# Two last output tiles: one 128-row store each in place of two 64-row stores

## The chip, the cores and the metric

The kernel runs on one core of one Trainium2 chip. The metric is device time in microseconds for one execution, as the median of several runs. The engines of the core have names of their own in the profile: PE is TensorE (matmuls), ACT is ScalarE, DVE is VectorE, POOL is GpSimd and SP is SyncE. SyncE and ScalarE each have a queue from which they issue transfers between the on-chip memory (SBUF) and device memory. The transfers are carried out by 16 DMA engines that the queues share.

## The reference

An attention block with sketched polynomial features is followed by a feed-forward block with the ELU activation. Only the last lines matter for the change, but the whole is short:

```python
# q, k, v: (4, 4, 1088, 32) float32; S1, S2: (8, 32)
def phi(x):                                   # 64 features from 32 numbers
    a = einsum('rd,bhsd->bhsr', S1, x)
    b = einsum('rd,bhsd->bhsr', S2, x)
    return einsum('bhsi,bhsj->bhsij', a, b).reshape(..., 64)
q_p, k_p = phi(q), phi(k)
kv = einsum('bhsf,bhsd->bhfd', k_p, v)
z = sum(k_p, axis=2)
attn = einsum('bhsf,bhfd->bhsd', q_p, kv) / (einsum('bhsf,bhf->bhs', q_p, z)[..., None] + 1e-06)

x = attn.transpose(0, 2, 1, 3).reshape(4352, 128)
h = x @ w_in                                  # w_in (128, 2048)
g = where(h > 0, h, exp(minimum(h, 0)) - 1)
out = g @ w_out                               # w_out (2048, 128), out (4352, 128) float32
```

## The kernel before

The 4352 rows of the output are held as 4 batches of 64 x 17 rows: row (b, y, t) with y from 0 to 63 and t from 0 to 16. A "half tile" is one (b, t), 64 rows that lie 17 rows apart in the output. There are 68 half tiles, in nine groups g of eight; the last group (g = 8) has only four. Its two output tiles of 128 rows are the last work of the kernel.

```python
NT = S // 64                                   # 17
NH = B * NT                                    # 68 half tiles
NQ = (NH + 7) // 8                             # 9 groups
qn = [min(8, NH - 8 * g) // 2 for g in range(NQ)]   # tiles of a group: 4, the last group 2

def half_tile(g, k):
    return divmod(8 * g + k, NT)
# ... cut ...
def halves(dst, lhs, rhs, **kw):               # one product as two matmuls of 64 output rows
    for u in range(2):
        nc.tensor.matmul(dst[64 * u:64 * u + 64], lhs[:, 64 * u:64 * u + 64], rhs, skip_group_check=True,
                         tile_position=(0, 64 * u), **kw)
# ... cut ...
def mm2_last(cp, first, last):                 # second product of the last group: rows on the partitions
    g = NQ - 1
    if first:
        ops[g] = [psum.tile([P, P], F32, name="ol", tag=t, bufs=k) for t, k in (("o0", 1), ("aux", 2))]
    gg = gs.pop((g, cp))
    for a in range(4):
        c, i = (a % 2, a // 2) if last else divmod(a, 2)
        halves(ops[g][i][:], gg[:, c, i * P:i * P + P], W[:, cp, (2 + c) * P:(3 + c) * P],
               start=(first and c == 0), stop=(last and c == 1))

def fin_last():                                # copy out of PSUM, and store
    g, n = NQ - 1, qn[NQ - 1]
    o = work.tile([P, 2, P], F32, name="ol", tag="ol", bufs=1)
    rows = out.rearrange("(b y t) f -> b y t f", b=B, t=NT)
    for i, copy in enumerate((nc.scalar.copy, nc.vector.tensor_copy)):
        copy(o[:, i, :], ops[g][i][:])
        for u, eng in enumerate((nc.sync, nc.scalar)):
            b, t = half_tile(g, u * n + i)
            eng.dma_start(rows[b, :, t, :], o[64 * u:64 * u + 64, i])
```

In the last step (cp = 7) the matmuls of tile i = 0 come before those of tile i = 1, so the first copy, on ScalarE, can begin while the second tile is still being summed. The earlier groups are stored by SyncE alone, from tiles named ob.

ScalarE issues only three other transfers, all at the start of the kernel. S2 goes to the tile raw_s, eight rows of 256 B. The second half of the first k goes to the tile hd_k, and a half of the first queries goes to hd_q:

```python
def load_hd(eng, x, src, b, t0, t1, c=slice(0, 2)):
    # ... cut ...
    eng.dma_start(hd[x, b][:, c, t0:t1, :],
                  src[b].rearrange("h (a c t) d -> (h a) c t d", a=32, c=2)[:, c, t0:t1, :])
# ... cut ...
for x, (eng, src) in enumerate(((nc.sync, S1), (nc.scalar, S2))):
    rs = slice(R * x, R * x + R)                             # R = 8
    # ... cut ...
    eng.dma_start(raw_s[rs].rearrange("p c w -> p (c w)"), src.bitcast(U32))
load_hd(nc.sync, "k", k, 0, 0, KT)                           # KT = 9
load_hd(nc.scalar, "k", k, 0, KT, NT)
load_hd(nc.sync, "q", q, 0, 0, 8, slice(0, 1))
load_hd(nc.scalar, "q", q, 0, 0, 8, slice(1, 2))
```

Of the kernel before, what the change touches and what calls it, by code (L numbers as in the profile page):

```python
# [27 lines left out]
def kernel(  # L28
# [21 lines left out]
    nc = tc.nc  # L50
# [413 lines left out]
    def half_tile(g, k):  # L464
        return divmod(8 * g + k, NT)
# [372 lines left out]
    def fin_last():  # L838
        g, n = NQ - 1, qn[NQ - 1]
        o = work.tile([P, 2, P], F32, name="ol", tag="ol", bufs=1)  # L840
        rows = out.rearrange("(b y t) f -> b y t f", b=B, t=NT)
        for i, copy in enumerate((nc.scalar.copy, nc.vector.tensor_copy)):
            copy(o[:, i, :], ops[g][i][:])
            for u, eng in enumerate((nc.sync, nc.scalar)):
                b, t = half_tile(g, u * n + i)
                eng.dma_start(rows[b, :, t, :], o[64 * u:64 * u + 64, i])


    for t0, t1 in ((0, 5), (KT, KT + 5), (5, KT), (KT + 5, NT)):
# [143 lines left out]
    for n in range(2, N + 2):  # L993
        if n < N:
            g, cp = steps[n]
# [26 lines left out]
        g, cp = steps[n - 2]  # L1022
# [5 lines left out]
        elif n > 2:  # L1028
            mm2(g, cp, cp == 0, cp == NP - 1)
            if cp == NP - 1:  # L1030
                fin1(g)
    fin_last()


# [27 lines left out]
```

## Time and profile before

| what | value |
|---|---|
| time, median of 3 runs | 268.3 us (267.77 to 268.83) |
| span of the profiled execution | 266.5 us |
| PE busy | 260.4 us, 98% |
| DVE busy | 187.7 us, 70% |
| ACT busy | 183.9 us, 69% |
| POOL busy | 159.6 us, 60% |
| DMA packets, whole run | 26418, 13.60 MB |
| of these on q1, SyncE's queue | 25792 |
| of these on q10, ScalarE's queue | 592 |

The profile is of one execution; its span is a little shorter than the time measured from outside. Times inside it are counted from the start of the span. A line such as L846 is the line of the kernel from which an instruction comes. In this kernel L843 is the copy in fin_last and L846 its store. SPq and ACTq are the instruction queues of SyncE and ScalarE, where issues of transfers and waits are seen. "To landing" is the time from the issue of a transfer to the last of its completion signals. A packet is one contiguous run that a DMA engine moves, or the small write by which it signals completion.

### The profile page before, as it was taken

The numbers are of one execution on the slowest core, as the hardware profiler recorded it, in microseconds if no ns is written. First come the engines' busy times: TensorE is split into PE (matmuls) and PEld (weight loads), VectorE is DVE, ScalarE is ACT, GpSimd is POOL, SyncE is SP. The second block draws the span as 40 slices with busy tenths as digits, with TensorE's granted clock in tenths as the row PEclk, the third lists the DMA queues.
The fourth block names the chain that finished last, engine by engine and source line by source line (L and its number), as shares of the span: only waits on it lengthen the run. The fifth ranks groups of instructions, "written<-read, shape, count | busy, mean of one in ns | idle before, by whom it ended". The sixth has DMA issues, their size and how long they took to land.

```text
span 266.5 us, 7686 instructions
## 1 busy us (share of the span) xinstructions
PE 260.4 (98%) x3115; PEld 154.9 (58%) x3115; DVE 187.7 (70%) x346; ACT 183.9 (69%) x355; POOL 159.6 (60%) x233
## 2 busy tenths in 40 slices
PE   8899999999999999999999999999999999999994
PEld 6743323343333665667576666666766666666884
DVE  6799999996969796996647867554346444673652
ACT  2378978686566575786567777777777777777782
POOL 4400007303505985798859799898688888898300
PEclk9999999999999999999999999999999999999999
DMA  5997960001001300001100110001000100010011
GB/s 192 320 349 215 270 197 17 0 21 65 2 0 28 57 1 2 2 2 19 27 5 0 21 22 2 0 12 25 10 1 15 27 4 1 14 19 12 2 27 35
DMA packets 26418, 13.60 MB, mean 51 GB/s; under 512 B 19216, under 2 KB 24592, under 8 KB 26384
## 3 DMA queue, kind: packets, MB, share of 16 engines
q1 hardware_dynamic: 25792, 12.66, 18.5%
q8 instruction: 24, 0.39, 0.6%
q10 hardware_dynamic: 592, 0.46, 0.5%
q14 instruction: 10, 0.08, 0.1%
HBM read 10.88 MB, written 2.23 MB: 49 GB/s over the span
## 4 chain that ended last, share of the span: by engine, by line
PE 93%; DVE 4%; POOL 1%; issue 1%; ACT 0%; DVEq 0%
PE h L226 43%; PE pb L730 16%; PE pa L730 12%; PE o L226 11%; PE ol L226 3%; PE idle L231 2%; PE kv L391 1%; PE h L648 1%; PE qps L648 1%; DVE qp L586 1%; POOL kp L287 1%; PE kfps L323 1%; PE qps L542 1%; PE kv L226 1%; PE abp L304 1%
## 5 line engine op out<-in xcount | busy, mean ns | idle before, releaser
L799 DVE SCALAR_TENSOR_TENSOR gg<-e,h 128x512 f32<-128x512 f32 (+1 forms) x144 | 92.3, 653 | 64.2 <-ACT e L793 62.9
L226 PE MATMUL h<-xg,W 128*64 128x512 f32 (+1 forms) x584 | 128.7, 563 | 0.0
L791 ACT ACTIVATE e<-h 128x512 f32<-128x512 f32 (+1 forms) x144 | 81.4, 565 | 50.6 <-PE h L226 48.1
L793 ACT ACTIVATE e<-e 128x512 f32<-128x512 f32 (+1 forms) x144 | 87.5, 607 | 4.4
L226 PEld LDWEIGHTS h<-xg,W 128*64 128x64 f32 x584 | 40.1, 137 | 47.4 <-issue 36.8
L710 POOL TENSOR_TENSOR tt<-gg 128x256 f32<-128x256 f32 x48 | 35.1, 730 | 16.4 <-DVE gg L799 16.0
L713 POOL TENSOR_TENSOR tt<-gg 128x256 f32<-128x256 f32 x48 | 35.3, 736 | 14.4 <-DVE gg L799 14.0
L715 POOL TENSOR_TENSOR tt<-gg,tt 128x256 f32<-128x256 f32 x48 | 36.5, 760 | 3.8
L714 POOL TENSOR_TENSOR tt<-tt,gg 128x256 f32<-128x256 f32 x48 | 35.2, 733 | 3.8
L730 PEld LDWEIGHTS pa<-gg,W 128*64 128x64 f32 x384 | 23.6, 137 | 22.7 <-issue 22.0
L226 PE MATMUL o<-gg,W 128*64 128x512 f32 x128 | 30.5, 597 | 0.4 <-DVE W L129 0.4
L730 PE MATMUL pa<-gg,W 128*64 128x128 f32 x384 | 29.5, 275 | 0.0
L730 PE MATMUL pb<-tt,SS 128*64 128x128 f32 x384 | 29.1, 273 | 0.0
L730 PEld LDWEIGHTS pb<-tt,SS 128*64 128x64 f32 x384 | 22.6, 137 | 0.0
L126 POOL TENSOR_TENSOR raw<-raw,tiny 128x512 f32<-128x512 f32 x1 | 1.0, 1039 | 29.8 <-DVE raw L121 29.8
L730 PE MATMUL pb<-gg,SS 128*64 128x128 f32 x192 | 18.7, 273 | 0.0
L730 PE MATMUL pa<-tt,SS 128*64 128x128 f32 x192 | 18.6, 273 | 0.0
L730 PE MATMUL pb<-tt,W 128*64 128x128 f32 x192 | 18.6, 273 | 0.0
L226 PEld LDWEIGHTS o<-gg,W 128*64 128x64 f32 x128 | 8.5, 136 | 16.2 <-issue 13.8
L730 PEld LDWEIGHTS pb<-tt,W 128*64 128x64 f32 x192 | 12.1, 137 | 0.0
L730 PEld LDWEIGHTS pa<-tt,SS 128*64 128x64 f32 x192 | 12.1, 137 | 0.0
L730 PEld LDWEIGHTS pb<-gg,SS 128*64 128x64 f32 x192 | 12.1, 137 | 0.1
(150 smaller groups left out, 245.0 us busy)
## 6 DMA issues: line engine op xcount, KB each, us to landing
raw<-in_moe_w_in_dram SPq DMA_DIRECT2D x8, 256.0 KB, 5.8
raw<-in_moe_w_out_dram SPq DMA_DIRECT2D x8, 256.0 KB, 5.8
hd_k<-in_k_dram SPq DMA_DIRECT2D x3, 544.0 KB, 7.8
hd_q<-in_q_dram SPq DMA_DIRECT2D x3, 544.0 KB, 3.2
v<-in_v_dram SPq DMA_DIRECT2D x4, 288.0 KB, 6.4
out_dram<-ob SPq DMA_DIRECT2D x72, 16.0 KB, 1.5
v<-in_v_dram SPq DMA_DIRECT2D x4, 256.0 KB, 7.5
out_dram<-ob SPq DMA_DIRECT2D x16, 32.0 KB, 1.7
```

Source lines behind the costliest of these rows:

```text
L226: nc.tensor.matmul(dst[64 * u:64 * u + 64], lhs[:, 64 * u:64 * u + 64], rhs, skip_group_check=True, tile_position=(0, 64 * u), **kw)
L231: nc.tensor.matmul(idle[:, :cols], some[:, :P], some[:, :cols], skip_group_check=True)
L287: eng.tensor_mul(dst, _ap(a_, list(a_.ap[1:]) + [[0, R]]), _ap(b_, [b_.ap[1], [0, R], b_.ap[2]]))
L648: nc.tensor.matmul(ps[w][s * r:s * r + s, 64 * k:64 * (k + m)], lhs, qpT[g, i][rows, o + 2 * k:o + 2 * (k + m), f, :], start=(f == 0 and j ...
L710: nc.gpsimd.tensor_tensor(t[:, 0], b12, b11, op=SUB)
L713: nc.gpsimd.tensor_tensor(t[:, 2], b22, b12, op=SUB)
L714: nc.gpsimd.tensor_tensor(t[:, 1], t[:, 2], b11, op=ADD)
L715: nc.gpsimd.tensor_tensor(t[:, 3], b21, t[:, 1], op=SUB)
L730: nc.tensor.matmul(bank[64 * u:64 * u + 64, P * col:P * col + P], lhs, rhs[:, u], start=(first and i in (0, 3)), stop=last, skip_group_che ...
L791: nc.scalar.activation(e, hs[g, cp][c][:, :n], RELU, scale=-1.0)
L793: nc.scalar.activation(e, e, EXP, scale=-1.0)
L799: nc.vector.scalar_tensor_tensor(gs[g, cp][:, c, :n], es[g, cp][:, c, :n], -1.0, hs[g, cp][c][:, :n], op0=ADD, op1=MAX)
```

## The change

Before, each of the two last tiles is stored in two halves of 64 rows, the half u = 0 by SyncE and the half u = 1 by ScalarE: four transfers, two on each queue. After, each tile is stored by one transfer of 128 rows: the first, which ScalarE has copied, by ScalarE, and the second, which VectorE has copied, by SyncE. Two issues on the two queues fall away, and SyncE has nothing in front of the last store. The two halves of a tile lie n = 2 values of t apart in the output, so the destination is written as (u, y, f), with u outermost.

```diff
         o = work.tile([P, 2, P], F32, name="ol", tag="ol", bufs=1)
         rows = out.rearrange("(b y t) f -> b y t f", b=B, t=NT)
-        for i, copy in enumerate((nc.scalar.copy, nc.vector.tensor_copy)):
+        for i, (copy, eng) in enumerate(((nc.scalar.copy, nc.scalar), (nc.vector.tensor_copy, nc.sync))):
             copy(o[:, i, :], ops[g][i][:])
-            for u, eng in enumerate((nc.sync, nc.scalar)):
-                b, t = half_tile(g, u * n + i)
-                eng.dma_start(rows[b, :, t, :], o[64 * u:64 * u + 64, i])
+            b, t = half_tile(g, i)
+            eng.dma_start(rows[b, :, t:t + n + 1:n, :].rearrange("y u f -> u y f"), o[:, i])
```

Nothing else in the kernel is changed.

## The prediction

> **What bounds the kernel now.** I read the profile's page first. It says that the matmul engine carries the run: 98% busy over the span, 93% of the chain that ended last. The change touches none of that. It only touches the last two stores, so the question is what lies between the last matmul and the end of the span, and whether the stores set that end. The chain of work in order of time, cut to the last microseconds, answers half of it (columns: start, duration, what):
>
> ```profile
> 260.32 2.64 PE ol L226 x48
> 262.96 0.02 issue
> 262.99 0.29 DVE ol L843
> ```
>
> The chain stops at the second copy, which ends at 262.99 + 0.29 = 263.28 us. The span ends at 266.5 us. So 3.2 us come after the last arithmetic. The timeline of the same stretch shows who starts the stores, and the sync engine's own waits show what it waits for after that (waited for: us in total, times, longest):
>
> ```profile
> 262.55 0.27 ACT L843 COPY ol<-ol 128x128 f32<-128x128 f32 x1 [1.06 <-PE ol L226]
> 262.84 1.19 SPq L846 DMA_DIRECT2D out_dram<-ol  x2
> 262.84 1.46 ACTq L846 DMA_DIRECT2D out_dram<-ol  x2
> ```
>
> ```profile
> SPq L1058 <- DMA out_dram<-ol: 1.4, 2, 1.2
> ```
>
> L1058 is the end of the program. SyncE sits there until the output transfers have landed. So the tail is store-bound: from the copies to the landing nothing else runs. The instructions on the tile ol give the issue cost and the landing:
>
> ```profile
> L846 SPq DMA_DIRECT2D out_dram<-ol x2: 542/545/548, 262.8 to 263.5; - x2
> L846 ACTq DMA_DIRECT2D out_dram<-ol x2: 562/683/804, 262.8 to 263.5; - x2
> ...
> DMA to landing us min/median/max: 1.9/2.1/2.1
> ```
>
> Last, the DMA view cut to 263.9 to 265.4 us, which is 40 slices of 37.5 ns (each digit the mean busy share of the 16 DMA engines):
>
> ```profile
> DMA  0000447763154796310003477631246963200000
> DMA packets 320, 0.13 MB, mean 88 GB/s; under 512 B 64, under 2 KB 320, under 8 KB 320
> q10 hardware_dynamic: 160, 0.07, 18.3%
> q1 hardware_dynamic: 160, 0.07, 18.0%
> ```
>
> There are four humps, one for each of the four 64-row transfers. They start in slices 4, 11, 21 and 28, that is at 264.05, 264.31, 264.69 and 264.95 us, and the last packet ends at about 265.25. Matched with the issues: a SyncE store (262.84 and about 263.5) moves its first data 1.2 us after its issue; a ScalarE store (same issue times) comes 1.45 to 1.5 us after. Each hump lasts 0.26 to 0.3 us. Between the last packet and the span's end lie 266.45 - 265.25 = 1.2 us, which I take as fixed.
>
> The packets matter most. Queue q10 is ScalarE's: 160 packets for two transfers is 80 each, 64 rows of 512 B and 16 completions of under 512 B. So each transfer was dealt over 16 engines, four rows on each. Its time: 18.3% of 16 engines over 1.5 us is 0.183 x 16 x 1.5 = 4.39 us. Over 2 x 16 engine shares that is 137 ns for four rows and a completion, so at most 34 ns a row.
>
> **What the Trainium skill says.** The page "DMA: Bandwidth & Descriptors", section "Why a DMA increments its semaphore by 16 and not by 1", says that a transfer issued by SyncE or ScalarE is spread over k engines, where k is the largest number up to 16 that divides the slowest dimension (not of size one) of both sides, and that it is the lowest-numbered k engines. Only those k post a completion. The trace agrees in what it can show. All of ScalarE's queue up to 240 us:
>
> ```profile
> q10 hardware_dynamic: 432, 0.40, 0.5%
> ```
>
> By the code these are three loads: k in runs of 1 KB (256 rows), a half of the first q tiles in runs of 1 KB (128 rows), and S2 (8 rows). With 16 completions for the first two, 432 - 272 - 144 = 16 packets are left for S2: 8 rows and 8 completions, not 24. A leading dimension of 8 took 8 engines. Which 8 cannot be seen.
>
> The same page's "Rules for kernel authors" advises one 128-partition transfer rather than two to disjoint halves, as both halves use the same engines. This is the idea of the change, and the trace agrees that halves take turns: two stores issued at the same moment made humps 0.26 us apart. But the advice presumes that the one transfer is spread over 16 engines.
>
> "Perfetto Trace Analysis", section "DMA Instruction — HWDGE (DVE, Sync)", says that an issue's reported duration excludes the data movement, and that the last completion waits until the write is confirmed. It agrees: issues of 0.54 to 0.8 us, landing after 1.9 to 2.1 us. So a longer transfer will not show in the issue rows.
>
> **The change part by part.**
>
> 1. Removed: two of four issues, one on each queue. Before, SyncE's first issue ran from 262.84 to 263.39, past the second copy's end at 263.28, so the second store began at about 263.5. Now SyncE is free and waiting, and can issue 25 ns after the copy, as ScalarE does after its own (262.55 + 0.265 = 262.815, issue at 262.84): at 263.30. Gain on the path: about 0.2 us. ScalarE's second issue, the one that landed last, is gone: it trailed SyncE's by another 0.26 us, but its rows now stand in SyncE's transfer.
>
> 2. Kept: the same 65,536 x 2 bytes, in the same 512 B rows, 256 rows in all. Matmuls, copies and earlier stores do not move; the order of instructions on every other engine is the same.
>
> 3. Changed shape: the destination is now (u = 2) x (y = 64) x 128 elements, and the source 128 partitions x 128. The slowest dimension of the destination is 2, where it was 64. By the skill's rule k falls from 16 to 2. Each of two engines gets 64 rows from each transfer, and both transfers use the same two: 128 rows and 2 completions per engine.
>
> 4. What that costs: at about 33 ns a row (the at most 34 above, less a little for the completion), 128 x 33 = 4.2 us. A lower estimate: in the loads from 9 to 14 us, by the table of busy time in windows, the DMA moved 359 GB/s at a share of 1.08, so 359 / 16 / 1.08 = 20.8 GB/s an engine, or 25 ns for 512 B: 128 x 25 = 3.2 us. A pair of engines without fourteen neighbours should lie between: I take 29.5 ns, 3.8 us.
>
> 5. On the path: ScalarE's store is issued at 262.84 with no SyncE store ahead of it, so first data comes at about 264.05. SyncE's joins at 263.30 + 1.2 = 264.5, long before the first is through, so the two engines stay busy from 264.05 on: last packet at 264.05 + 3.8 = 267.85. Before it was 265.25. The gain of part 1 is swallowed, because the engines, not the issue, now decide. Sum: +2.6 us (between +2.0 and +3.1 for 25 to 33 ns). The time becomes 268.3 + 2.6 = 270.9 us, 1.0% longer.
>
> **The rivals.**
>
> Spread over 16 after all: if the hardware treats the 128 rows as one dimension, the last store moves data from 263.30 + 1.2 = 264.5 for two humps' length, 0.55 us, and ends at 265.05: 0.2 us gained, 268.1 us. For it: the source side does have 128 partitions. Against it: S2's 8 completions show that a leading dimension does decide. I give it one in ten.
>
> Two engines each, but not the same two: then each engine has only 64 rows, the last store ends at 264.5 + 64 x 0.0295 = 266.4, and the cost is 1.15 us: 269.45 us. Nothing in the trace speaks for it, the skill's rule speaks against; one in ten.
>
> A long run on one engine is slower than short ones: the trace has no store with more than eight rows to an engine in one transfer, and a writer that waits for confirmations, or a descriptor buffer that fills, could show only now. At 45 ns a row: 5.8 us, +4.5 us, 272.8. To lose 2% (5.4 us), the run must take 1.2 + 5.4 = 6.6 us, 51 ns a row, half as much again as anything averaged here.
>
> A matmul-side rival, that the stores disturb or release something earlier, has no ground: both stores come after the last matmul.
>
> **Range and chances.** The centre is 270.9. The low end, 269.3, takes in separate pairs of engines; the high end, 272.5, takes in 42 ns a row. Outside are full spreading (268.1) below, and a rate above 42 ns above. The three runs before lie 0.5 us around their median, which the range also has to hold. Faster by over 2% would need 5.4 us, more than the whole 3.2 us tail: one in a hundred. Slower by over 2%: six in a hundred. The rest is within 2%.
>
> **What would show it.** In the changed profile ScalarE's queue should hold 592 - 160 + 64 x 2 + 2 = 562 packets (576 if 16 engines), and SyncE's 25792 - 160 + 130 = 25762 (25776). After 264.05 us the DMA share should stand at or below 2/16 = 0.125 for 3.2 to 4.2 us, in one flat stretch in place of four humps. The landing should take about 4.5 us for both stores instead of 1.9 to 2.1. SyncE's store should be issued at about 263.3, and the copies should end as before. The prediction is wrong if the packet counts show 16 completions, or if the stretch is much shorter (different engines) or longer (a slow long run) than 3.8 us.

## The result and the profile after

The changed kernel takes 270.37 us (median of 6 runs, 269.95 to 270.84), the kernel before on the same chip 268.07 us (267.77 to 268.83). The ratio is 1.0084, with a 95% interval from 1.0066 to 1.0102: 2.3 us longer, where 2.6 us were predicted.

The timeline of the end shows that nothing ahead of the stores has moved (columns: start, duration, engine, line, operation):

```profile
262.57 0.27 ACT L843 COPY ol<-ol 128x128 f32<-128x128 f32 x1 [1.06 <-PE ol L226]
262.87 0.66 ACTq L845 DMA_DIRECT2D out_dram<-ol  x1
263.01 0.29 DVE L843 COPY ol<-ol 128x128 f32<-128x128 f32 x1 [1.04 <-PE ol L226]
263.33 0.63 SPq L845 DMA_DIRECT2D out_dram<-ol  x1
```

The second copy ends at 263.01 + 0.29 = 263.30 us, 0.02 us later than before. SyncE issues its store 30 ns after it, where before it was still busy with its first store until 263.39 and issued the second at about 263.5. This part of the change does what it is for. But the span now ends at 268.7 us, so 5.4 us follow the last copy, where it was 3.2. SyncE's waits say where they go (waited for: us in total, times, longest):

```profile
SPq L1057 <- DMA out_dram<-ol: 3.6, 2, 2.2
```

It was 1.4 us before. The DMA view of the changed kernel, cut to 263.9 to 267.9 us (40 slices of 100 ns), shows what the end of the program waits for:

```profile
DMA  0001011111111101111111111111111111100000
GB/s 0 0 20 20 20 26 41 46 46 41 41 31 31 41 15 46 41 46 41 46 41 41 46 41 46 41 46 41 46 41 46 41 46 41 46 21 0 0 0 0
DMA packets 260, 0.13 MB, mean 33 GB/s; under 512 B 4, under 2 KB 260, under 8 KB 260
q10 hardware_dynamic: 130, 0.07, 6.2%
q1 hardware_dynamic: 130, 0.07, 5.4%
```

The four humps have become one low, flat stretch, from 264.15 to 267.5 us, mostly at 41 to 46 GB/s where the humps went up to 232 GB/s. Each store has 128 rows and 2 completions; four packets under 512 B in all, where there were 64. Two engines carry each store. The page gives the same for the whole run, in the very numbers that were expected of two engines:

```profile
q1 hardware_dynamic: 25762, 12.66, 18.4%
...
q10 hardware_dynamic: 562, 0.46, 0.5%
```

### The profile page after: what moved, and what is told of

The parts are those of the page before. It is cut to its first block, busy times and chain, and to the rows that moved or that the text cites. A ratio compares the mean times of both kernels' runs of the same rounds, so it can differ in the third digit from the quotient of the medians.

```text
span 268.7 us, 7682 instructions
## 1 busy us (share of the span) xinstructions
PE 259.3 (97%) x3115; PEld 154.1 (57%) x3115; DVE 187.3 (70%) x346; ACT 184.0 (68%) x355; POOL 159.8 (59%) x233
## 3 DMA queue, kind: packets, MB, share of 16 engines
q1 hardware_dynamic: 25762, 12.66, 18.4%
## 4 chain that ended last, share of the span: by engine, by line
PE 90%; DVE 4%; DMA 2%; issue 1%; ACTq 0%; ACT 0%; DVEq 0%
PE h L226 42%; PE pb L730 16%; PE pa L730 12%; PE o L226 11%; PE ol L226 3%; DMA hd_q<-in_q_dram 2%; PE kv L391 1%; PE h L648 1%; PE qps L648 1%; DVE qp L586 1%; PE kfps L323 1%; PE qps L542 1%; PE kv L226 1%; DVE qT L244 1%; DVE raw L121 0%
## 5 line engine op out<-in xcount | busy, mean ns | idle before, releaser
L730 PE MATMUL pa<-gg,W 128*64 128x128 f32 x384 | 29.5, 274 | 0.0
```

What stands on the lines that cost most here:

```text
L730: nc.tensor.matmul(bank[64 * u:64 * u + 64, P * col:P * col + P], lhs, rhs[:, u], start=(first and i in (0, 3)), stop=last, skip_group_che ...
```

## The experiments

Theory: the slowest dimension of the destination, u = 2, puts each store on two engines, and both stores meet on the same pair. A store's rows divided by its engines then set the end. Rivals: a store of 128 rows is slow in any order; the new roles of the two queues cost the time; a store in progress holds up the next as a whole.

Since runs differ by some tenths in when the matmuls end, the profiles are compared by their tail: from the end of the second copy to the end of the span. Before it is 3.2 us, after 5.4 us. Each group of experiments has its own runs of the kernel before on the same chip, 267.68 us for the first four and 268.02 us for the last three, so times are compared by their ratio.

### The same stores with y outermost (e1_y_first)

ScalarE's copy that brings the last input tile into place deals its columns so that partition 2y + u of the output tile holds row (y, u). Then the same 128-row store can name its destination with y outermost. Matmuls, copies, issues and bytes stay as in the changed kernel.

```diff
--- after
+++ e1_y_first
-                nc.scalar.copy(x[:, :2 * n].rearrange("p (k w s) -> p w k s", w=2, s=64)[:, w],
-                               ps[w][:, :n].rearrange("p (k s) -> p k s", s=64))
+                nc.scalar.copy(x[:, :2 * n].rearrange("p (k h w l) -> p w k h l", k=2, w=2, l=1)[:, w],
+                               ps[w][:, :n].rearrange("p (k h l) -> p k h l", k=2, l=1))
...
-            eng.dma_start(rows[b, :, t:t + n + 1:n, :].rearrange("y u f -> u y f"), o[:, i])
+            eng.dma_start(rows[b, :, t:t + n + 1:n, :], o[:, i])
```

> The same two 128-row stores on the same two queues, but the destination written with y (64) outermost and u (2) inside; the columns of the last input tile are dealt to match (partition 2y + u). Theory (the leading dimension of 2 put each transfer on two DMA engines): 16 completions a transfer again, ScalarE's queue 576 packets, the data stretch shrinks from 3.3 us to about 1.1 us, span about 266.3 us, time about 267.9 us, 0.1% below the kernel before. Rival (a single transfer of 128 rows is slow by itself, whatever its order, or the pair of queues is to blame): the stretch stays above 2.5 us and the time at about 270.4 us.

Measured: 267.57 us beside 267.68 us for the kernel before, ratio 0.9999 (0.9987 to 1.0011). The DMA view of this kernel from 263.2 to 264.7 us (slices of 37.5 ns):

```profile
DMA  0000000367998642000035799954100000000000
DMA packets 288, 0.13 MB, mean 87 GB/s; under 512 B 32, under 2 KB 288, under 8 KB 288
q10 hardware_dynamic: 144, 0.07, 15.2%
q1 hardware_dynamic: 144, 0.07, 15.0%
```

Two humps, one for each store, are all done in 22 slices, 0.83 us. Each store has 128 rows and 16 completions. The rival, that a 128-row store is slow in itself, falls: the order of dimensions, with the dealing of rows that goes with it, is worth the whole 2.3 us. The timeline of the end gives the tail:

```profile
262.36 0.29 DVE L843 COPY ol<-ol 128x128 f32<-128x128 f32 x1 [1.05 <-PE ol L226]
262.68 0.63 SPq L845 DMA_DIRECT2D out_dram<-ol  x1
```

With a span of 265.6 us that is 265.6 - 262.65 = 2.95 us, about 0.2 us less than before, which is what the early issue promised. That is one profile of each kernel. The whole time does not show it: 0.2 us is less than 0.1%, and the interval reaches 0.13% below. So this version takes the loss away but is not shown to beat the kernel before.

### One store at a time (e2_first_only, e3_last_only)

```diff
--- before
+++ e2_first_only (e3_last_only: i == 1)
-        for i, copy in enumerate((nc.scalar.copy, nc.vector.tensor_copy)):
+        for i, (copy, eng) in enumerate(((nc.scalar.copy, nc.scalar), (nc.vector.tensor_copy, nc.sync))):
             copy(o[:, i, :], ops[g][i][:])
+            if i == 0:
+                b, t = half_tile(g, i)
+                eng.dma_start(rows[b, :, t:t + n + 1:n, :].rearrange("y u f -> u y f"), o[:, i])
+                continue
             for u, eng in enumerate((nc.sync, nc.scalar)):
```

> Only the first tile is stored by one transfer with u outermost (by ScalarE); the second by two 64-row halves as before. Theory (two engines are busy, the other fourteen free): the 128-row store takes 64 rows x 23.5 ns = 1.5 us on its two engines, from 264.07 to about 265.7; SyncE's half of the second tile starts at about 264.5 on the other engines and ends when the two busy engines are through, last packet about 265.9, span about 267.1, time about 268.8 us. Rival (a transfer in progress holds up the next one as a whole, as the changed profile hints, where the second store began only when the first was done): no packet of SyncE's store before 265.6, last packet 266.2, span 267.4, time about 269.1 us.

Measured: 268.9 us beside 267.68, ratio 1.0044 (1.0031 to 1.0058), 1.2 us longer. The tail, from the second copy's end at 262.94 + 0.29 = 263.23 us to the span's end at 267.3 us, is 4.1 us, 0.9 more than before. The DMA view of e2 from 263.9 to 267.4 us (slices of 87.5 ns), and then of the same kernel from 264.0 to 265.5 us:

```profile
DMA  0011111111243789411111100000000000000000
q10 hardware_dynamic: 210, 0.10, 9.9%
q1 hardware_dynamic: 80, 0.03, 5.8%
```

```profile
q10 hardware_dynamic: 182, 0.09, 20.3%
q1 hardware_dynamic: 70, 0.03, 12.5%
```

The hump in the middle stands on the flat stretch: the two 64-row stores, SyncE's and then ScalarE's, run on the other engines while ScalarE's large one goes on. By 265.5 us 70 of SyncE's 80 packets have moved. Ten are left: eight rows and two completions, which is just the part of two engines out of sixteen. The last data come in slice 22, at about 265.9 us, as the theory said. The time does not decide between theory and rival (0.7 and 1.0 us more than the 268.07 us of the kernel before were expected, 1.2 was measured); SyncE's packets before 265.5 us do. A store in progress does not hold up the next one as a whole; it holds up what falls on its own engines.

> Only the second tile is stored by one transfer with u outermost (by SyncE); the first by two 64-row halves as before. Theory: first tile done at 264.6 as before; the second is issued at about 263.5, starts at 264.7 and needs 64 rows x 23.5 ns plus 0.15 us on its two engines, last packet about 266.35, span about 267.55, time about 269.2 us (+1.1). Rival (only two large transfers meeting on the same pair cost anything): as before, 268.1 us.

Measured: 269.18 us beside 267.68, ratio 1.0057 (1.004 to 1.0074), 1.5 us longer; the tail is 267.4 - 263.19 = 4.2 us, 1.0 more than before. The DMA view of e3 from 263.9 to 267.4 us:

```profile
DMA  0598300011111111111111111100000000000000
q1 hardware_dynamic: 210, 0.10, 10.5%
q10 hardware_dynamic: 80, 0.03, 3.3%
```

The humps of the first tile come and go, and the second tile's store then runs flat for 18 slices, 1.6 us, with nothing beside it. So two large stores need not meet: one alone costs about 1 us of tail. Both together cost 2.2, close to the sum of 0.9 and 1.0, as work that stands in line on the same engines should.

### The queues alone (e4_queues)

```diff
--- before
+++ e4_queues
-        for i, copy in enumerate((nc.scalar.copy, nc.vector.tensor_copy)):
+        for i, (copy, eng) in enumerate(((nc.scalar.copy, nc.scalar), (nc.vector.tensor_copy, nc.sync))):
             copy(o[:, i, :], ops[g][i][:])
-            for u, eng in enumerate((nc.sync, nc.scalar)):
+            for u in range(2):
```

> The other half of the change alone: four 64-row stores as before, each over 16 engines, but both halves of the first tile from ScalarE and both of the second from SyncE, so that SyncE is free at the second copy. Theory: SyncE issues at 263.30 and about 263.9 instead of 262.84 and 263.5; its second store starts 1.2 us later at 265.1 and ends at about 265.4, against 265.25 before: time 268.1 to 268.4 us, not to be told from before. Rival (the reassignment of the queues is what costs): over 269 us.

Measured: 268.26 us beside 267.68, ratio 1.0019 (1.0009 to 1.003), 0.5 to 0.6 us longer. The tail is 266.9 - 263.41 = 3.5 us, 0.3 more than before. The timeline of the end:

```profile
262.97 1.20 ACTq L846 DMA_DIRECT2D out_dram<-ol  x2
263.12 0.29 DVE L843 COPY ol<-ol 128x128 f32<-128x128 f32 x1 [1.05 <-PE ol L226]
263.43 1.19 SPq L846 DMA_DIRECT2D out_dram<-ol  x2
```

SyncE needs 1.19 us to issue two stores one after the other after the last copy, where before the two queues issued one each. That is a small, real loss, not the same as before, though below the 269 us of the rival. It cannot be the cause of the 2.3 us: in the changed kernel SyncE has only one store to issue, and e1_y_first keeps the new queues without the loss.

### Other numbers of engines (e5_y63, e6_y57, e7_y61)

These three take e1_y_first and store fewer of the 64 values of y, so that the slowest dimensions of the two sides share other divisors. They leave rows of the output out: 2, 14 and 6 of the 128 in each of the two tiles.

```diff
--- e1_y_first
+++ e5_y63 (e6_y57: :57 and :114; e7_y61: :61 and :122)
-            eng.dma_start(rows[b, :, t:t + n + 1:n, :], o[:, i])
+            eng.dma_start(rows[b, :63, t:t + n + 1:n, :], o[:126, i])
```

> As the order with y outermost, but only 63 of the 64 values of y are stored (126 rows a store, two rows of each tile left out of the output), so that the two sides' slowest dimensions are 126 and 63, with 9 the largest common divisor up to 16. Theory (that divisor is the number of engines): 9 completions a store, 14 rows an engine, first to last packet about 0.9 us, no longer than with 16 engines. Rival (the number of engines must be a power of two): 1 completion and 5.9 us or more.

> As before it, with 57 values of y (114 rows a store, fourteen rows of each tile left out). Largest common divisor of 114 and 57 up to 16: 3. Theory: 3 completions a store, 38 rows an engine and store, 76 x 23.5 ns plus the 0.3 us lost at the start: first to last packet about 2.1 us. Rival (a power of two): 1 completion and 5.4 us or more.

> As before it, with 61 values of y (122 rows a store, six rows of each tile left out). 122 and 61 share no divisor up to 16 but 1. Theory: 1 completion a store, all 244 rows on one engine, 244 x 23.5 ns plus 0.3 us: first to last packet about 6.0 us, time about 273 us, with fewer rows stored than in any other kernel here. Rival (uneven rows are spread by the remainder): under 2 us.

The packets of ScalarE's queue over the whole run, in e5, e6 and e7 in turn:

```profile
q10 hardware_dynamic: 567, 0.46, 0.5%
```

```profile
q10 hardware_dynamic: 549, 0.45, 0.5%
```

```profile
q10 hardware_dynamic: 555, 0.46, 0.5%
```

The 432 packets of the earlier loads and the rows of the one store (126, 114, 122) leave 9, 3 and 1. The number of completions is the largest common divisor up to 16 each time, and it need not be a power of two. The rate fits as many engines. With three completions, the DMA view of e6 from 263 to 267 us (slices of 100 ns) settles at 61 to 67 GB/s, where the changed kernel, with two, has 41 to 46:

```profile
GB/s 0 0 0 0 36 31 56 41 72 56 51 61 77 46 51 41 36 67 61 61 67 67 67 61 51 10 0 0 0 0 0 0 0 0 0 0 0 0 0 0
```

Here are the five kernels of this form by the number of engines, with first to last packet read from cuts of the DMA view and the tail from timeline and span. Between e1 and the changed kernel only the order of dimensions differs, with the dealing of rows; the other three store fewer rows. The ratio of e7 rests on two runs.

| engines a store | kernel | rows on one engine, both stores | first to last packet | tail | ratio to before |
|---|---|---|---|---|---|
| 16 | e1_y_first | 16 | 0.83 us | 2.95 us | 0.9999 (0.9987 to 1.0011) |
| 9 | e5_y63 | 28 | 1.1 us | 3.5 us | 1.0007 (0.9973 to 1.004) |
| 3 | e6_y57 | 76 | 2.1 us | 4.4 us | 1.0046 (1.003 to 1.0062) |
| 2 | changed kernel | 128 | 3.3 us | 5.4 us | 1.0084 (1.0066 to 1.0102) |
| 1 | e7_y61 | 244 | 6.7 us | 8.9 us | 1.0225 (1.0152 to 1.0298) |

From 28 rows to 244 the stretch grows by 5.6 us, which is 26 ns a row. At 16 engines the rows of an engine no longer set the stretch: 16 x 26 = 0.42 us, and the two stores are simply 0.47 us apart in issue. The kernel with nine engines was expected at 0.9 us, no longer than with sixteen; it took 1.1 us, and its tail is 0.55 us longer. The kernel with one engine was expected at 6.0 us of stretch and about 273 us. It took 6.7 us, and 273.9 us beside 268.02. Its DMA view from 264 to 272 us (slices of 200 ns) shows a slow patch early on:

```profile
GB/s 0 0 5 5 10 20 23 15 20 23 10 8 3 8 20 23 20 23 20 23 20 23 20 23 20 23 20 23 20 23 20 23 20 23 20 18 0 0 0 0
```

One engine moves 20 to 23 GB/s when it runs smoothly, but only 3 to 8 in the first two slices with data and in the three from 266.2 to 266.8 us. These stalls, longer here than with two engines, are the missing 0.7 us. What they are was not tried.

## Why the prediction was right

**What bounds the end.** Right. The tail belongs to the stores, and the chain up to the second copy is unchanged: it ended at 263.28 us before and at 263.30 after. The 1.2 us from last packet to span's end is the same, 267.5 to 268.7 us.

**The earlier issue** (part 1, 0.2 us gained). Right in the profile: SyncE issued at 263.33 us. Where nothing swallows the gain, the tail is shorter by about as much (2.95 us in e1_y_first for 3.2), but it is too small to be seen in the measured time.

**Two engines** (part 3). Right, by the completions: 562 and 25762 packets. The Trainium skill's rule on the number of engines in "DMA: Bandwidth & Descriptors" ("Why a DMA increments its semaphore by 16 and not by 1") agreed with the trace for five values, 16, 9, 3, 2 and 1. That both stores use the same engines is shown by the sums of e2 and e3, and by the ten packets that SyncE's store left for the pair in e2. Which two engines they are, no run shows.

**The time of a row** (part 4). This is the term that was mis-sized. I took 29.5 ns a row, 3.8 us for 128 rows. It was 3.3 us, 26 ns a row, start included. Once in motion it is less, as the DMA view of the changed kernel from 266.2 to 267.2 us shows:

```profile
DMA packets 85, 0.04 MB, mean 44 GB/s; under 512 B 0, under 2 KB 85, under 8 KB 85
q1 hardware_dynamic: 85, 0.04, 14.3%
```

85 rows in 1 us on two engines is 23.5 ns a row. The DMA share of 14.3% is over 2/16 = 12.5%, so that the records of consecutive rows on one engine overlap: 0.143 x 16 / 85 us = 27 ns each, begun every 23.5. Busy time divided by rows, as I took it from the short humps, is therefore more than the pace of a long run. The lower estimate, 25 ns from the loads, in which engines were kept full, was the better one. The guess that the share stays at or below 0.125 was wrong for the same reason. The first data came 0.1 us later than predicted, at 264.15 us: 264.15 + 3.3 + 1.2 gives a span of 268.65 us, where 268.7 was measured. (At the upper end, 33 ns a row, the predicted sum is +3.0 us, not +3.1.)

**The order on the pair** (part 5). Wrong, without effect on the sum. I had SyncE's store join at 264.5 us and both stores land after about 4.5 us. The DMA view of the changed kernel from 264.0 to 265.85 us holds none of SyncE's packets:

```profile
DMA packets 120, 0.06 MB, mean 33 GB/s; under 512 B 0, under 2 KB 120, under 8 KB 120
q10 hardware_dynamic: 120, 0.06, 12.7%
```

Cut at 265.93 us the view holds 127 packets, all of them ScalarE's still. So SyncE's first row came only when 127 of the 128 of ScalarE's store had begun, 2.6 us after its issue. Since the end needs both, the sum is the same as with turns.

**The rivals.** Full spreading did not happen, and separate pairs would have given 269.45 us and a tail of 4.35 us, not 5.4. A slow long run fell too, for two engines: the long run went at 26 ns a row, start included, not at 45. With one engine the early stalls added 0.7 us.

## What to carry to other kernels

Merging two stores into one saves an issue, but it can cost far more if the merged access pattern puts a short dimension outermost: two stores of 128 rows took 3.3 us on 2 engines and 0.83 on 16. Before merging, look at the slowest dimension of both sides and count the completion packets in the profile afterwards; if the merge needs a small dimension, put it inside, by dealing rows to partitions in that order in a copy that is made anyway. And at the end of a kernel this shows in full, because nothing is left to hide a store behind: 0.13 MB there cost 2.3 us.

## What I had not expected of the hardware

Two stores on the same engine from two queues did not take turns from the start. In the changed kernel nearly all of the first went ahead. In the kernel with one engine, SyncE issued 0.46 us after ScalarE, yet the DMA view from 264.3 to 267.0 us and then from 267.0 to 269.25 us has:

```profile
DMA packets 67, 0.03 MB, mean 13 GB/s; under 512 B 0, under 2 KB 67, under 8 KB 67
q10 hardware_dynamic: 67, 0.03, 5.8%
```

```profile
q10 hardware_dynamic: 52, 0.03, 3.9%
q1 hardware_dynamic: 44, 0.02, 3.3%
```

A cut at 267.18 us holds 75 rows of ScalarE's store and still none of SyncE's. So 75 rows went alone, and only then did the queues alternate, one for one (47 and 46 from 267.2 to 269.4 us). Together they moved no faster than one alone, 96 rows in 2.25 us or 23.4 ns a row, as on one shared engine. Whether the engine takes a first batch of one queue before it looks at the other, or SyncE's rows reached it late, is open.

The issue itself took longer in the three kernels with fewer rows: 0.60 and 0.63 us with 16, 0.93 and 0.92 us with 9, 0.87 and 0.86 us with 3, but 0.66 and 0.63 us with 2 and 0.76 us with 1. Whether the number of engines or the number of rows makes the difference was not tried. With 9 engines the first data also came later, 1.54 us after ScalarE's issue (262.36 to 263.9) for 1.25 us with 16 (262.21 to 263.46). The longer issue accounts for it: counted from the issue's end it is 0.61 and 0.65 us. The 0.29 us are about half of the 0.55 us by which the tail of e5_y63 is longer; the other half is its longer stretch.
